# Packed attention and two MoE layers on one core: each engine's order of steps read from a table, the first batch's second-attention result split from SBUF, the coefficients loaded later

## The chip, the cores and the metric

One core of a Trainium2 chip runs the kernel. The metric is device time in microseconds (us), the median of three runs. The core has five engines that run their own instruction streams: PE (matmul, with weight loads listed as PEld), ACT, DVE, POOL and SP. In this kernel SP computes nothing: it issues the DMAs, one after the other, and a DMA whose data isn't there yet holds up all that stand behind it.

## The reference, cut to what matters

```python
batch, n_heads, seq, head_dim, n_pack = 8, 8, 576, 64, 32
n_tokens, d_model, d_ff = 4608, 512, 2048

def sm_attn(qq, kk, vv):
    s = scale * qq @ kk.T
    a = exp(s - max(s));  a = a / (sum(a) + 1e-09)
    return a @ vv

p_packed = sm_attn(p, k, v)                 # 32 rows a head
out = sm_attn(q, p_packed, p_packed)        # 576 rows a head
x = out.transpose(0, 2, 1, 3).reshape(4608, 512)

h = x @ w_in1                               # layer 1, w float64
P = a[0] + a[1]*h + a[2]*h**2 + a[3]*h**3
Q = 1 + |b[0]|*|h| + |b[1]|*h**2
x = (P / (Q + 1e-06)) @ w_out1

h = x @ w_in2                               # layer 2
out = (h * cos(h)) @ w_out2
```

## The kernel before

The attention is cut into 16 units (8 batches, two groups of four heads). A unit u transposes k, q and p on PE, makes the first softmax and from it the packed values, then the second softmax, whose weights, turned, stand in SBUF as `a2T` and are written to DRAM (`keep_attn`). The second product of the attention isn't made: `m_prod` multiplies the packed values into layer 1's `w_in` and gives a matrix M for a batch, so layer 1 starts from the softmax weights themselves.

Layer 1 runs over items j = 0 to 127: 16 half-batches c of 288 rows, eight items each. A product in float32 is made of three matmuls with operands split in a high and a low part (`..._hi` on ACT, `..._lo` on POOL or DVE). For each half-batch `a2_load` (L742) brings the softmax weights back from DRAM by two DMAs, one for each head group, `a2_hi` (L749, ACT) and `a2_lo` (L753, POOL) split them. Then for each item: `front` (L815, PE, 12 matmuls into one of two PSUM buffers `b`), `lin`, `absolute`, `slope` (ACT, L930, L944, L947), `cubic` (DVE, L939, L941), `denom` (POOL, L953), `log` and `inverse` (ACT, L956 and the next), `over` and `ratio` (DVE, L964, L968), `upper` (ACT, L996: the high part gh), `lower` (DVE, L999: the low part gl), and `back` (L852, PE, `acc<-gh,wo` and `acc<-gl,wo`). `front(j)` must wait until `cubic(j-2)` has read the PSUM buffer.

Layer 2 runs over items j = 128 to 271: nine chunks of 512 rows, 16 items each: `front` (L831), `lin` (L932), `rounded`, `reduced`, `clipped` (DVE, L972, L977, L979, L983), `cosine` (ACT), `times` (DVE, L990, the last reader of the PSUM buffer), `upper`, `lower`, and `back` (L852) in four steps m = 0 to 3. Its operand x comes from layer 1's output through DRAM: `x_load` (L895) and `x_rest` (L904) load the two sums of it, `x_sum` (POOL, L911) adds them, `x_hi` (L914, ACT) and `x_lo` (L918, DVE) split. Finished rows go by `done2` and `store` (L883).

The weights are float64 and come in as words: `w_load` (SP, L420, L425, L430), `w_exp` (L438) and `w_low` (L441, ACT), `w_abs` (L447) and `w_join` (L457, DVE), `w_hi` (L464, ACT), `w_lo` (L469, POOL). Layer 2's split `w_in` is written to DRAM (`keep_out`, L473) and loaded again (`w_back`, L476) while layer 1 ends, so weights of layer 2 are made beside the last items of layer 1.

What sets the order: every step is given to `plan.add` with its engine, its estimated length and what it reads and writes. `Plan.order` (L165 on) is a list scheduler: at each turn it takes, on the engine that can start first, that ready step with the least key among those that can start within 60 ns; a key is a sum of numbers found by tuning (`FIRST`, `EACH`, `WANTED`, `SHIFT`, by kind of step and place). Some steps also have to start behind others for the order alone (`after=`). The engines then get their instructions in this order, and semaphores keep the data right whatever the order is. The coefficients `par` (a[0..3], b[0..1]) are loaded by two DMAs ahead of everything (L1191, L1192).

Of the kernel before, what the change touches and what calls it, by code (L numbers as in the profile page):

```python
# [29 lines left out]
class Plan:  # L30
# [14 lines left out]
    WANTED = {  # L45
        "a2_hi": 1434, "a2_lo": 1536, "a2_load": -474, "absolute": -10, "absolute E": 828,
        "back 0": 407, "back 0 E": 574, "back 0 late E": 528, "back 1": 689, "clipped": 16,
        "copied k": 171, "copied k late": -117, "copied q": 61, "copied q late": 11, "cosine": -71,
# [3 lines left out]
        "exp_copied": -162, "exp_copied late": 137, "front 0": -336, "front 0 E": -21,  # L52
        "front 1": -170, "inverse": -79, "inverse E": 445, "keep_attn": -41, "keep_attn late": 15,
        "keep_out": 8, "keep_pack": -20, "keep_pack late": 229, "less_max2": -238,
        "less_max2 late": 87, "lin 0": 478, "lin 0 E": -611, "lin 1": -42, "load k": -478,
        "load k late": 78, "load p": -265, "load p late": -150, "load q": 49, "load q late": -161,
        "load v": -40, "load v late": -161, "log": 130, "log E": 244, "lower 0": -197,
        "lower 0 E": -245, "lower 1": 42, "m_hi": 793, "m_lo": -878, "m_load": 210, "m_prod": -188,
        "max1": -207, "max1 late": -84, "max2": -89, "max2 late": -237, "open_both": -151,
        "open_left": 19, "open_right": 88, "over 0": 25, "over 0 E": -124, "over 1": 23,  # L60
        "over 1 E": 120, "pack": 484, "pack late": 835, "packed": -18, "packed late": 191,
        "ratio": -8, "ratio E": -597, "recip1": 67, "recip1 late": 532, "recip2": 20,
        "recip2 late": 135, "reduced 0": -127, "reduced 1": -19, "rounded": 168, "scaled2": 114,
        "scaled2 late": 586, "scores 0": -176, "scores 0 late": -509, "scores 1": -379,
        "scores 1 late": -439, "slope": -18, "slope E": 518, "store": 300, "sum2": 80,
        "sum2 late": 1506, "taken p": -187, "taken p late": -160, "taken pp": 86,
        "taken pp late": -281, "times": -192, "trans k": -2, "trans k late": -333, "trans q": 692,
        "trans q late": -11, "turn2": -113, "turn2 late": -446, "turn_back": -189,
        "turn_back late": 1932, "turn_exp": 172, "turn_exp late": 219, "turned p": 73,
        "turned p late": 358, "turned pp": 24, "turned pp late": 59, "upper 0": 104,  # L70
# [13 lines left out]
    FIRST = {
        "i": 220.69, "j": 453.76, "k": 1649.06, "u": -144.84, "v": 113.95, "wi": -3610.16,
        "wi late": -1623.51, "wo": 597.92, "wo late": -1411.71,
    }
    EACH = {
        "i": 5.11, "j": 0.57, "k": 0.82, "u": -0.29, "v": 13.86, "wi": 0.11, "wi late": -1.42,
        "wo": -0.76, "wo late": -0.9,  # L90
    }
    SHIFT = {
# [63 lines left out]
    @staticmethod  # L156
    def kind(name, args):
        if name[:2] == "w_" and len(args) == 3:
            return f"{name} {args[0]} {args[2]}"
        if name in ("cubic", "over", "reduced", "trans", "copied", "turned", "taken", "load", "scores"):  # L160
            return f"{name} {args[1]}"
        if name in ("front", "back", "lin", "upper", "lower"):
            return f"{name} {int(args[0] >= 128)}"
        return name
# [1074 lines left out]
```

## Time and profile before

| | us |
|---|---|
| median of 3 runs (range) | 1619.49 (1619.04 to 1621.25) |
| the profiled execution | 1621.15 |
| its span, first to last instruction | 1619.4 |
| PE busy | 1553.7 (96%) |
| DVE busy | 1293.7 (80%) |
| ACT busy | 1032.1 (64%) |
| POOL busy | 344.0 (21%) |

The profiled execution lasts 1.75 us longer than its span and 1.66 us longer than the median. All rows below come from it. Lines L... are lines of the kernel before. In a timeline row the first number is the start (us from the span's start), the second the length of the group of instructions, then engine, line, operation, the tiles written and read, the shape and the number of instructions; the brackets give the idle time just before on that engine and what ended it. The program's parts follow in time: attention alone to some 65 us, attention and layer 1 to 150 us, layer 1 to about 800 us with layer 2's weights beside its last fifth, layer 2 from about 815 us.

### The profile page before, as it was taken

Reading aid. Unit: us, or ns where it says so; the run is one execution under the profiler, and the core shown is the slowest. Engines: PE = TensorE matmul, PEld = TensorE weight load, DVE = VectorE, ACT = ScalarE, POOL = GpSimd, SP = SyncE. Lnnn points to the kernel's source line nnn. Section 1 sums busy time; section 2 is a strip of 40 time slices with the busy share of each in tenths; the row PEclk is TensorE's granted clock in tenths of the full one; section 3 lists DMA queues with packets and bytes.
Section 4 is the critical chain, followed back from the end, with each engine's and each line's share of the span. In section 5 each row is a group of like instructions: output and inputs, shape, how many; then the busy total and the mean of one; then the engine's idle time right before and its main releaser. Section 6 shows DMA issues by size and latency. Waiting matters only on the chain.

```text
span 1619.4 us, 26741 instructions
## 1 busy us (share of the span) xinstructions
PE 1553.7 (96%) x10128; PEld 1335.3 (82%) x10128; DVE 1293.7 (80%) x2025; ACT 1032.1 (64%) x1745; POOL 344.0 (21%) x274
## 2 busy tenths in 40 slices
PE   5888998999999999999989999999999999999998
PEld 4566898789999999999878888888888788888887
DVE  4799999999999999998889876676676667666664
ACT  6898999989998888998767433333333333333332
POOL 1454442433343333333323100000000000000000
PEclk9999999999999999999999999999999999999999
DMA  9994115321221211134653310201010101010010
GB/s 307 334 318 152 63 48 168 102 75 50 74 80 52 67 64 62 43 104 139 200 161 119 82 35 13 53 20 46 14 39 14 39 1 43 10 31 22 1 27 27
DMA packets 98881, 133.61 MB, mean 83 GB/s; under 512 B 20928, under 2 KB 75712, under 8 KB 98752
## 3 DMA queue, kind: packets, MB, share of 16 engines
q1 hardware_dynamic: 98368, 131.38, 26.1%
q8 instruction: 80, 1.31, 0.3%
q10 hardware_dynamic: 384, 0.52, 0.1%
q14 instruction: 49, 0.40, 0.1%
HBM read 94.11 MB, written 37.75 MB: 81 GB/s over the span
## 4 chain that ended last, share of the span: by engine, by line
PE 76%; DVE 9%; ACT 8%; DMA 3%; issue 2%; POOL 2%; SPq 0%; DVEq 0%; POOLq 0%; ACTq 0%
PE acc L852 39%; PE b L831 24%; PE b L815 9%; PE b L765 2%; PE b L539 1%; DVE gl L999 1%; DVE T L964 1%; DMA raw<-in_moe_w_in_dram 1%; DMA k_in<-in_k_dram 1%; ACT T L930 1%; POOL U L953 1%; DVE T L941 1%; DVE T L939 1%; DVE T L968 1%; DVE U L964 1%
## 5 line engine op out<-in xcount | busy, mean ns | idle before, releaser
L852 PE MATMUL acc<-gh,wo 128*128 128x288 f32 x2048 | 420.1, 299 | 6.6 <-ACT ob L865 3.7
L852 PE MATMUL acc<-wo,gh 128*128 128x512 f32 x1152 | 354.9, 389 | 0.2
L852 PEld LDWEIGHTS acc<-gh,wo 128*128 128x128 f32 x2048 | 329.6, 189 | 29.6 <-issue 13.5
L852 PE MATMUL acc<-gl,wo 128*128 128x288 f32 x1024 | 302.6, 296 | 2.5 <-DVE gl L999 2.5
L953 POOL TENSOR_TENSOR U<-U,V 128x576 f32<-128x576 f32 x128 | 184.0, 1446 | 337.1 <-DVE T L964 90.6
L852 PEld LDWEIGHTS acc<-wo,gh 128*128 128x128 f32 x1152 | 216.0, 188 | 45.7 <-DVE xr L873 0.8
L932 ACT ACTIVATE T<-b 128x512 f32<-128x512 f32 x144 | 86.1, 598 | 219.2 <-PE b L831 218.4
L852 PE MATMUL acc<-wo,gl 128*128 128x512 f32 x576 | 224.4, 390 | 0.8 <-DVE gl L999 0.8
L999 DVE TENSOR_TENSOR gl<-V,gh 128x512 fp32r<-128x512 f32 x144 | 99.4, 690 | 122.5 <-PE acc L852 118.3
L852 PEld LDWEIGHTS acc<-gl,wo 128*128 128x128 f32 x1024 | 194.0, 189 | 3.5 <-DVE gl L999 3.5
L987 ACT ACTIVATE U<-U 128x512 f32<-128x512 f32 x144 | 90.8, 630 | 156.9 <-DVE U L983 156.8
L996 ACT CAST gh<-V 128x512 fp32r<-128x512 f32 x144 | 89.5, 621 | 76.3 <-PE acc L852 70.9
L972 DVE TENSOR_SCALAR T<-T 128x512 f32<-128x512 f32 x144 | 62.8, 436 | 91.2 <-ACT T L932 91.0
L852 PEld LDWEIGHTS acc<-wo,gl 128*128 128x128 f32 x576 | 108.1, 188 | 24.1 <-DVE gl L999 1.7
L947 ACT ACTIVATE U<-V,par 128x576 f32<-128x576 f32 x128 | 111.4, 870 | 1.3 <-DVE T L968 1.0
L990 DVE TENSOR_TENSOR V<-U,b 128x512 f32<-128x512 f32 x144 | 98.4, 684 | 17.2 <-ACT U L987 13.4
L999 DVE TENSOR_TENSOR gl<-T,gh 128x576 fp32r<-128x576 f32 x128 | 108.1, 846 | 4.5 <-PE acc L852 2.4
L930 ACT ACTIVATE T<-b,par 128x576 f32<-128x576 f32 x128 | 105.7, 831 | 4.8 <-PE b L815 4.0
L979 DVE SCALAR_TENSOR_TENSOR U<-T,U 128x512 f32<-128x512 f32 x144 | 105.2, 730 | 3.4
L964 DVE SCALAR_TENSOR_TENSOR U<-U,V 128x576 f32<-128x576 f32 x128 | 100.1, 786 | 8.0 <-POOL xr L911 4.3
L941 DVE SCALAR_TENSOR_TENSOR T<-T,par,b 128x576 f32<-128x576 f32 x128 | 102.0, 810 | 4.3 <-ACT V L944 1.7
L964 DVE SCALAR_TENSOR_TENSOR T<-T,par,V 128x576 f32<-128x576 f32 x128 | 105.1, 823 | 0.1
(182 smaller groups left out, 3077.3 us busy)
## 6 DMA issues: line engine op xcount, KB each, us to landing
raw<-in_moe_w_out_dram SPq DMA_DIRECT2D x32, 512.0 KB, 3.6
raw<-in_moe_w_in_dram SPq DMA_DIRECT2D x30, 512.0 KB, 4.6
x<-ob SPq DMA_DIRECT2D x24, 576.0 KB, 3.5
k_in<-in_k_dram SPq DMA_DIRECT2D x16, 576.0 KB, 7.4
q_in<-in_q_dram SPq DMA_DIRECT2D x16, 576.0 KB, 6.6
v_in<-in_v_dram SPq DMA_DIRECT2D x16, 512.0 KB, 7.2
w<-sc SPq DMA_DIRECT2D x32, 256.0 KB, 2.9
xr<-a SPq DMA_DIRECT2D x48, 144.0 KB, 3.4
```

Of the source, the lines that this page charges most:

```text
L815: nc.tensor.matmul(TILE["h", j][:, e, 0:HS], lhsT=w[:, o : o + P], rhs=x[:, g, :], start=n == 0, stop=n == 3 * NG - 1,)
L831: nc.tensor.matmul(h, lhsT=w[:, ks], rhs=x, start=n == 0, stop=n == 3 * KC - 1)
L852: nc.tensor.matmul(o, lhsT=w, rhs=x, start=i == first and n == 0, stop=i == last and n == len(todo) - 1,)
L930: nc.scalar.activation(T, hidden(j), AF.Identity, scale=par[:, 3:4], bias=par[:, 2:3])
L941: nc.vector.scalar_tensor_tensor(T, T, par[:, 1:2], h, op0=ALU.add, op1=ALU.mult)
L947: nc.scalar.activation(shaped(j, "U"), shaped(j, "V"), AF.Identity, scale=par[:, 5:6], bias=par[:, 4:5])
L953: return nc.gpsimd.tensor_tensor(Q, Q, V, op=ALU.mult)
L964: return nc.vector.scalar_tensor_tensor(t, t, add_, shaped(j, "V"), op0=ALU.add, op1=ALU.mult)
L979: return nc.vector.scalar_tensor_tensor(Y, T, -C2, Y, op0=ALU.mult, op1=ALU.add)
L987: nc.scalar.activation(Y, Y, AF.Sin, bias=PI/2)
L990: nc.vector.tensor_tensor(shaped(j, "V"), shaped(j, "U"), hidden(j), op=ALU.mult)
L999: return nc.vector.tensor_tensor(shaped(j, "gl"), result(j), shaped(j, "gh").bitcast(F32), op=ALU.subtract)
```

## The change

`Plan.order` no longer chooses: five lists of step numbers, `ORDER`, say for PE, ACT, DVE, POOL and SP which step comes next, and the loop only finds which slot each new tile gets. The keys and their numbers go, and so do those `after=` that were there for the order alone. The lists are near the old order, with steps moved singly. Three things change beside the order:

- `par_load` (two DMAs) and `par_abs` (ACT) become steps with a place in the lists. On SP they stand behind the first two weight loads, two p loads and two k loads.
- For the first batch (half-batches 0 and 1, first pass) `part_hi` and `part_lo` split the softmax weights from `a2T` in SBUF, 288 columns of one head group at a time. The four DMAs of `a2_load` for them, two `a2_hi` and two `a2_lo` of 576 columns go; four `part_hi` and four `part_lo` come. The store `keep_attn` remains.
- `logs[-1]` is now `inverse`, so that the cosine, which needs another function table on ACT, is put behind the last `inverse` and not the last `log`.

```diff
-    WANTED = {
-        "a2_hi": 1434, "a2_lo": 1536, "a2_load": -474, "absolute": -10, "absolute E": 828,
...
+    ORDER = {
+        "PE": """
+7 9 11 47 13 45 49 51 17 19 85 25 55 87 21 27 57 23 63 83 59 30 123 65 89 125 161 121 163 159
...
-        (group, i, off), s.kind = key, self.kind(fn.__name__, args) + late
-        s.base = (group, i, off)
-        key = self.FIRST[group] + self.EACH[group] * i + off + self.WANTED.get(s.kind, 0)
...
+        turn = {e: [self.steps[int(n)] for n in t.split()] for e, t in self.ORDER.items()}
+        turn["-"] = [s for s in self.steps if s.eng == "-"]
+        at = dict.fromkeys(turn, 0)
...
-                at = [(may(s), s) for s in ws]
-                first = min(a for a, _ in at)
-                if first == inf:
-                    continue
-                a, s = min(((a, s) for a, s in at if a <= first + self.WINDOW), key=lambda x: (x[1].key, x[1].n))
...
+                a = may(ss[at[e]])
+                if a < inf and (best is None or a < best[0]):
+                    best = (a, ss[at[e]])
...
+    def of_half(c, g):
+        return TILE["a2T", g][:, (c % 2) * HS : (c % 2 + 1) * HS]
+
+    def part_hi(c, g):
+        nc.scalar.copy(a2_parts(c, 0)[0][:, g, :], of_half(c, g))
+
+    def part_lo(c, g):
+        hi, lo = a2_parts(c, 0)
+        return nc.gpsimd.tensor_tensor(lo[:, g, :], of_half(c, g), hi[:, g, :].bitcast(F32), op=ALU.subtract)
...
+    def par_load():
+        nc.sync.dma_start(par[:, 0:4], rat_a.unsqueeze(0).to_broadcast([P, 4]))
+        nc.sync.dma_start(par[:, 4:6], rat_b.unsqueeze(0).to_broadcast([P, 2]))
...
-        if a == 0 or c < CE:
+        if b == 0 and a == 0:
+            for g in range(NG):
+                home = dict(w=[("a2", c, 0)]) if g else dict(new=[("a2", ("a2", c, 0), [P, 2, NG, HS], F32R)])
+                add("ACT", 290, at(j, -20), part_hi, c, g, tail=100, r=[("a2T", g)], **home)
+                add("POOL", 740, at(j, -20), part_lo, c, g, r=[("a2T", g)], w=[("a2", c, 0)])
+        elif a == 0 or c < CE:
...
-        add("ACT", 585, key, inverse, j, tail=100, w=[("V", j)])
+        logs[-1] = add("ACT", 585, key, inverse, j, tail=100, w=[("V", j)])
...
-    nc.sync.dma_start(par[:, 0:4], rat_a.unsqueeze(0).to_broadcast([P, 4]))
-    nc.sync.dma_start(par[:, 4:6], rat_b.unsqueeze(0).to_broadcast([P, 2]))
```

The order of the fronts on PE is as before; their places among the other PE steps shift by one to three steps on average. Three places are shown here. In the rows stand line, operation, tile written, tiles read and size; the numbers in the names tell one use of a buffer from another, and the lines of the changed code are other lines.

POOL near the end of layer 1 (some 790 to 805 us). L469, later L698, is `w_lo`; L953, later L1192, is `denom`; L911, later L1150, is `x_sum`. U1_10271 before and U1_10284 after belong to `denom(125)`. Before:

```order
L953 TENSOR_TENSOR U2_10163<-U2_10163,V2_10137 128x576
L469 TENSOR_TENSOR sc1_10378<-sc0_10256,sc2_10330 128x512
L911 TENSOR_TENSOR xr0_10053<-xr0_10053,xq_10259 128x512
L953 TENSOR_TENSOR U1_10271<-U1_10271,V1_10226 128x576
L953 TENSOR_TENSOR U0_10340<-U0_10340,V0_10313 128x576
L911 TENSOR_TENSOR xr1_10380<-xr1_10380,xq_10414 128x512
```

And now:

```order
L1192 TENSOR_TENSOR U0_10175<-U0_10175,V2_10167 128x576
L1192 TENSOR_TENSOR U1_10284<-U1_10284,V0_10262 128x576
L698 TENSOR_TENSOR sc0_10359<-sc1_10234,sc2_10356 128x512
L1150 TENSOR_TENSOR xr0_10294<-xr0_10294,xq_10229 128x512
L1192 TENSOR_TENSOR U2_10353<-U2_10353,V1_10297 128x576
L1150 TENSOR_TENSOR xr1_10051<-xr1_10051,xq_10399 128x512
```

`denom(125)` has moved ahead of one `w_lo` and one `x_sum`.

SP from about 813 us, where layer 2 begins. L473, later L702, is `keep_out`; L476, later L705, is `w_back`; L430, later L659, is `w_load` of layer 2's `w_out`; L895 and L904, later L1134 and L1143, are `x_load` and `x_rest`; L1107 is `x_out`. Before:

```order
L476 DMA m11h_10552<-w2_14_167 128x1024
L430 DMA raw1_10578<-in_moe2_w_out_dram 128x512
L473 DMA w2_15_168<-sc2_10576 128x512
L473 DMA w2_15_168<-sc1_10580 128x512
L476 DMA m11l_10635<-w2_15_168 128x1024
L895 DMA xr1_10662<-x20_1_130 128x64
L895 DMA xr1_10662<-x20_2_131 128x288
L895 DMA xr1_10662<-x20_3_132 128x160
L904 DMA xq_10674<-x21_1_146 128x64
L904 DMA xq_10674<-x21_2_147 128x288
L904 DMA xq_10674<-x21_3_148 128x160
L430 DMA raw0_10685<-in_moe2_w_out_dram 128x512
```

And now:

```order
L659 DMA raw1_10578<-in_moe2_w_out_dram 128x512
L1143 DMA xq_10595<-x21_1_146 128x64
L1143 DMA xq_10595<-x21_2_147 128x288
L1143 DMA xq_10595<-x21_3_148 128x160
L702 DMA w2_15_168<-sc2_10576 128x512
L702 DMA w2_15_168<-sc0_10601 128x512
L659 DMA raw0_10674<-in_moe2_w_out_dram 128x512
L659 DMA raw1_10698<-in_moe2_w_out_dram 128x512
L1107 DMA x20_15_144<-ob_10625 128x4x288
L705 DMA s6_10710<-w2_6_159 128x1024
```

Before, the load of `w2_15` (the row into m11l) stands straight behind the stores of it, and the next `w_out` load behind that and six x loads. Now the next two `w_out` loads follow the stores at once, and the load of `w2_15` stands twelve steps of the list later.

DVE at the same place. L447, later L676, is `w_abs`; L457, later L686, is `w_join`; L979, later L1218, and L983, later L1222, are `reduced` and `clipped` of item 129; L999 is `lower(128)`; L990, later L1229, is `times(129)`. Before:

```order
L979 SCALAR_TENSOR_TENSOR U0_10622<-T1_10611,U0_10622 128x512
L447 SCALAR_TENSOR_TENSOR sc1_10637<-sc0_10600,sc1_10637 128x512
L999 TENSOR_TENSOR gl0_10668<-V1_10632,gh0_10646 128x512
L457 SCALAR_TENSOR_TENSOR sc1_10637<-raw0_10491,sc1_10637 128x512
L983 TENSOR_SCALAR U0_10622<-U0_10622 128x512
L447 SCALAR_TENSOR_TENSOR sc0_10670<-sc2_10666,sc0_10670 128x512
L457 SCALAR_TENSOR_TENSOR sc0_10670<-raw1_10578,sc0_10670 128x512
L990 TENSOR_TENSOR V0_10690<-U0_10622,b2_1_10582 128x512
```

And now:

```order
L1218 SCALAR_TENSOR_TENSOR U2_10635<-T1_10616,U2_10635 128x512
L676 SCALAR_TENSOR_TENSOR sc0_10648<-sc1_10606,sc0_10648 128x512
L1222 TENSOR_SCALAR U2_10635<-U2_10635 128x512
L686 SCALAR_TENSOR_TENSOR sc0_10648<-raw0_10454,sc0_10648 128x512
L676 SCALAR_TENSOR_TENSOR sc1_10669<-sc2_10666,sc1_10669 128x512
L1229 TENSOR_TENSOR V1_10677<-U2_10635,b2_1_10582 128x512
```

`lower(128)` and one `w_join` have moved behind `times(129)`, and `clipped(129)` ahead of a `w_join`.

## Rows read from the trace of the kernel before

**Rows 1.** The page: busy time of each engine; the chain that ended last, by engine.

```profile
PE 1553.7 (96%) x10128; PEld 1335.3 (82%) x10128; DVE 1293.7 (80%) x2025; ACT 1032.1 (64%) x1745; POOL 344.0 (21%) x274
...
PE 76%; DVE 9%; ACT 8%; DMA 3%; issue 2%; POOL 2%; SPq 0%; DVEq 0%; POOLq 0%; ACTq 0%
```

**Rows 2.** Stretches: us, busy PE, PEld, DVE, ACT, POOL, PE clock, DMA share, GB/s.

```profile
10.40:50.00 39.60, 32.45 (x457) 21.73 (x465) 25.19 (x55) 29.69 (x61) 6.76 (x13) 0.96 1.05 339
50.00:100.00 50.00, 42.14 (x680) 29.04 (x664) 39.76 (x81) 44.49 (x89) 24.84 (x26) 1.00 1.02 344
100.00:150.00 50.00, 41.06 (x541) 32.05 (x541) 45.74 (x87) 44.75 (x86) 23.89 (x21) 0.97 0.69 234
150.00:350.00 200.00, 186.72 (x1473) 168.86 (x1473) 191.05 (x263) 181.33 (x298) 77.28 (x57) 0.98 0.27 85
350.00:750.00 400.00, 397.97 (x3105) 379.73 (x3104) 383.67 (x514) 364.74 (x590) 144.69 (x103) 1.00 0.23 75
750.00:850.00 100.00, 90.76 (x556) 83.17 (x555) 86.10 (x124) 73.44 (x123) 34.84 (x26) 0.97 0.51 164
850.00:1500.00 650.00, 648.45 (x2835) 527.85 (x2834) 450.31 (x780) 252.41 (x432) 30.98 (x26) 1.00 0.14 36
```

**Rows 3.** Stretches of 10 us in which the granted clock of PE is low.

```profile
280.00:290.00 10.00, 4.58 (x28) 3.13 (x28) 10.00 (x14) 8.21 (x13) 4.16 (x3) 0.71 0.38 127
...
800.00:810.00 10.00, 7.67 (x44) 7.44 (x45) 6.60 (x9) 3.52 (x6) 4.18 (x4) 0.83 0.46 151
```

**Rows 4.** Timeline, the start: coefficients, packs, first matmuls.

```profile
0.74 0.40 SPq L1191 DMA_DIRECT2D par<-in_moe_a_dram  x1
...
4.34 1.50 SPq L517 DMA_DIRECT2D p_in<-in_p_dram  x2
...
10.43 3.41 PE L539 MATMUL b<-ident,k_in 128*128 128x128 f32 x14 [10.43 <-DMA k_in<-in_k_dram]
```

**Rows 5.** DMA issues on the page: tiles, count, KB each, us to landing.

```profile
k_in<-in_k_dram SPq DMA_DIRECT2D x16, 576.0 KB, 7.4
...
xr<-a SPq DMA_DIRECT2D x48, 144.0 KB, 3.4
```

**Rows 6.** Timeline, 54 to 78 us: the first half-batch's split and first front.

```profile
66.47 1.40 POOL L753 TENSOR_TENSOR a<-xr,a 128x576 fp32r<-128x576 f32 x1 [4.00 <-ACT a L749]
...
69.32 0.53 PE L815 MATMUL b<-a,m00h 128*128 128x288 f32 x2
```

**Rows 7.** Groups by line and form: count, busy us, mean ns of one.

```profile
L749 ACT CAST a<-xr 128x576 fp32r<-128x576 f32 x24 | 16.2, 680 | 0.0
...
L865 ACT ACTIVATE ob<-acc 128x288 f32<-128x288 f32 x96 | 38.9, 409 | 3.7 <-PE acc L852 3.3
...
L753 POOL TENSOR_TENSOR a<-xr,a 128x576 fp32r<-128x576 f32 x24 | 34.4, 1433 | 23.8 <-PE acc L852 5.0 <-ACT a L749 4.0 <-DVE U L964 3.8
...
L469 POOL TENSOR_TENSOR wo<-sc,wo 128x512 fp32r<-128x512 f32 x32 | 41.1, 1289 | 83.3 <-DVE sc L457 17.5 <-ACT wo L464 11.9 <-DVE sc L447 10.2
```

**Rows 8.** Timeline, 275 to 290 us: the front of item 31.

```profile
285.42 0.82 PE L815 MATMUL b<-a,m00h 128*128 128x288 f32 x2 [5.50 <-DVE T L941]
```

**Rows 9.** Timeline, 790 to 836 us: from layer 1 to layer 2.

```profile
794.07 1.99 POOL L953 TENSOR_TENSOR U<-U,V 128x576 f32<-128x576 f32 x1
...
801.55 0.53 PE L852 MATMUL acc<-gh,wo 128*128 128x288 f32 x2 [2.77 <-ACT gh L996]
...
812.56 0.68 DVE L918 TENSOR_TENSOR a<-xr,a 128x512 fp32r<-128x512 f32 x1
...
825.97 0.98 PE L831 MATMUL b<-a,s 128*128 128x512 f32 x3 [1.66 <-DVE V L990]
...
830.00 0.66 ACT L438 ACTIVATE sc<-raw 128x512 f32<-128x512 f32 x1 [3.44 <-DMA raw<-in_moe_w_out_dram]
...
833.87 1.65 PE L831 MATMUL b<-a,s 128*128 128x512 f32 x3 [2.12 <-DVE V L990]
```

**Rows 10.** Timeline, the end: the last store.

```profile
1615.71 0.85 SPq L883 DMA_DIRECT2D out_dram<-xr  x2
```

More of the change, by code (lines that the diff above doesn't have):

```diff
@@ L43 @@
     RING, ISSUE = 8, 480
-    WANTED = {
-        "a2_hi": 1434, "a2_lo": 1536, "a2_load": -474, "absolute": -10, "absolute E": 828,
-        "back 0": 407, "back 0 E": 574, "back 0 late E": 528, "back 1": 689, "clipped": 16,
-        "copied k": 171, "copied k late": -117, "copied q": 61, "copied q late": 11, "cosine": -71,
[3 rows of a table removed]
[L52 to L70, printed above, removed]
[10 rows of a table removed]
-        "w_low 1 o": 16, "x_hi": 597, "x_lo": 263, "x_load": -65, "x_out": 179, "x_out E": 87,
-        "x_rest": 278, "x_sum": -47,
-    }
@@ L84 @@
[L84 to L92, printed above, removed]
[13 rows of a table removed]
-    }
-    PER = {"i": 4, "j": 8}
+    ORDER = {
+        "PE": """
[80 rows of a table added]
+""",
+        "ACT": """
[88 rows of a table added]
+""",
+        "DVE": """
[102 rows of a table added]
+""",
+        "POOL": """
[14 rows of a table added]
+""",
+        "SP": """
[18 rows of a table added]
@@ L154, in add @@
         return s
[L156 to L164, printed above, removed]
     def order(self):
         free = dict.fromkeys(("PE", "ACT", "DVE", "POOL", "SP", "-"), 0)
-        wait = {e: [] for e in free}
+        turn = {e: [self.steps[int(n)] for n in t.split()] for e, t in self.ORDER.items()}
+        turn["-"] = [s for s in self.steps if s.eng == "-"]
+        at = dict.fromkeys(turn, 0)
         free |= {"behind DVE": 0, "behind POOL": 0}
@@ L175, in order @@
         head = dict.fromkeys(self.slots_of, 0)
-        for s in self.steps:
-            if not s.left:
-                wait[s.eng].append(s)
         done = []
@@ L200, in order @@
             best = None
-            for e, ws in wait.items():
-                if not ws:
+            for e, ss in turn.items():
+                if at[e] == len(ss) or ss[at[e]].left:
                     continue
-                at = [(may(s), s) for s in ws]
-                first = min(a for a, _ in at)
-                if first == inf:
-                    continue
-                a, s = min(((a, s) for a, s in at if a <= first + self.WINDOW), key=lambda x: (x[1].key, x[1].n))
-                if best is None or a < best[0]:
-                    best = (a, s)
-            assert best, [(s.fn.__name__, s.args) for ws in wait.values() for s in ws][:40]
+                a = may(ss[at[e]])
+                if a < inf and (best is None or a < best[0]):
+                    best = (a, ss[at[e]])
+            assert best, [(s.fn.__name__, s.args) for e, ss in turn.items() for s in ss[at[e] : at[e] + 1]]
             a, s = best
-            wait[s.eng].remove(s)
+            at[s.eng] += 1
             s.start = a
             if s.eng == "SP":
-                n, at = s.busy // self.ISSUE, a
+                n, begin = s.busy // self.ISSUE, a
                 for _ in range(n):
-                    at = max(at, landed[-self.RING])
-                    bus = max(bus, at + 600) + s.bus / n
+                    begin = max(begin, landed[-self.RING])
+                    bus = max(bus, begin + 600) + s.bus / n
                     landed.append(bus + 1400)
-                    at += self.ISSUE
-                s.end, free["SP"] = bus + 1400, at
+                    begin += self.ISSUE
+                s.end, free["SP"] = bus + 1400, begin
             elif s.bus:
@@ L253, in order @@
                 t.left -= 1
-                if not t.left:
-                    wait[t.eng].append(t)
             done.append(s)
@@ L485, in convert @@
         bus = 1700 if x[::2] == (1, "i") else 1340
-        t = add("SP", 960 if (l, which) == (0, "i") and f % NPR == NPR - 1 else 480, (group, n, off - 4), w_load, *x, late=late, new=[("raw", ("raw", *x), [P, 2 * DM], U32)], bus=bus, after=[*after, *last_load[0]])
+        t = add("SP", 960 if (l, which) == (0, "i") and f % NPR == NPR - 1 else 480, (group, n, off - 4), w_load, *x, late=late, new=[("raw", ("raw", *x), [P, 2 * DM], U32)], bus=bus)
         last_load[0] = (t,)
@@ L1067, in operands1 @@
                     add("DVE", 1140, key, m_lo, b, n, g, tail=85, r=[("mps", b, n, g), ("M", b, n, g, "h")], w=[("M", b, n, g, "l")])
-        if a == 0 or c < CE:
+        if b == 0 and a == 0:
[4 more added lines that the diff above has]
+        elif a == 0 or c < CE:
             x = half(c, a * HALF)
-            add("SP", 960, at(j, -60), a2_load, c, x, r=[("a2 out", b * NG + g) for g in range(NG)], new=[("xr", ("a2r", c, x), [P, NG, HS], F32)], bus=880, after=[fronts[j - 7]] if j > 7 else ())
+            add("SP", 960, at(j, -60), a2_load, c, x, r=[("a2 out", b * NG + g) for g in range(NG)], new=[("xr", ("a2r", c, x), [P, NG, HS], F32)], bus=880)
             add("ACT", 570, at(j, -20), a2_hi, c, x, tail=100, r=[("a2r", c, x)], new=[("a2", ("a2", c, x), [P, 2, NG, HS], F32R)])
@@ L1085, in item1 @@
         add("ACT", 545, key, absolute, j, tail=95, r=[("h", j)], new=[("V", ("V", j), *W2P)])
-        add("ACT", 730, key, lin, j, tail=100, r=[("h", j)], new=[("T", ("T", j), *W2P)])
-        add("ACT", 760, key, slope, j, tail=105, r=[("V", j)], new=[("U", ("U", j), *W2P)])
+        add("ACT", 730, key, lin, j, tail=100, r=[("h", j), ("par",)], new=[("T", ("T", j), *W2P)])
+        add("ACT", 760, key, slope, j, tail=105, r=[("V", j), ("par",)], new=[("U", ("U", j), *W2P)])
         add("DVE", 665, key, cubic, j, 0, tail=85, r=[("h", j)], w=[("T", j)])
```

16 lines of the change are left out of this document (9 added, 7 removed), and 327 rows, old and new, of tables (ORDER, SHIFT, WANTED).

## The prediction

> **What bounds the kernel now.** I read the engines' shares first: PE is busy 1553.7 of 1619.4 us, so at most 65.7 us could be won by filling its gaps, and the chain that ended last runs through PE for 76% [rows 1]. Then the stretches, since such a share is a mean over parts with different limits [rows 2]. PE's idle time is each stretch less its busy time: 7.15, 7.86 and 8.94 us in the three stretches from 10.4 to 150 us (23.95 in all), 13.28 from 150 to 350, 2.03 from 350 to 750, 9.24 from 750 to 850, and 1.55 in the 650 us of layer 2. The start (10.4 us before PE's first matmul [rows 4]) and the tail hold the rest.
>
> Three different limits show. From 10 to 100 us the DMA engines are full (share 1.05 and 1.02, 339 and 344 GB/s). From 150 to 750 us DVE is nearly full too: 191.05 + 383.67 = 574.7 of 600 us, so it has 25.3 us to spare, 4%. Layer 2 is PE's alone. [...]
>
> **The change part by part.** The sum is made against the profiled execution, 1621.15 us; the median is 1.66 below it.
>
> *Start, 0 to 10.4 us.* The coefficients leave SP's front; two p loads take their place ahead of the k loads. PE's first matmul waits for k until 10.43. Two coefficient loads take some 0.8 us of SP (0.40 for the first), two p loads 1.50 [rows 4], so k is issued 0.7 us later, or its data come 0.7 to 1 us earlier if the order in which the bytes travel decides. The coefficients are needed by the first `lin`, past 69 us, so their delay is covered by 60 us. I take 0; bounds -1 to +0.9.
>
> *First batch's split.* Out go four DMAs of 144 KB, 0.58 MB: at 342 GB/s that is 1.7 us of a stream that is full. Each took 3.4 us to land [rows 5], a wait that the first split no longer has. In come instructions of half the width. ACT: one of 576 columns takes 680 ns, one of 288 (the nearest row is the eviction) 409; so 2 x 409 - 680 = 0.14 us more for each of two half-batches, 0.28 us. POOL: 1433 ns at 576 and 1289 at 512 columns give 2.25 ns a column, so 785 ns at 288, and 2 x 785 - 1433 = 0.14, 0.27 us for both [rows 7]. POOL is 50% busy there; ACT is 89% busy, so up to 0.28 us of it may show. The front that reads this split started at 69.32 with no wait noted, the split having ended at 67.87 [rows 6]: the shorter path alone wins nothing on PE, since the front keeps its place in PE's list. What is won is the DMA stream's 1.7 us, where loads of q, k and v end PE's waits.
>
> [...]
>
> *Order, 10 to 150 us.* All other steps shift singly by a few places. The 23.95 us are many waits of under 1.5 us: for q, k, v from DMA, for ACT's evictions. A list that fits can take a part, while the DMA stream sets a floor: it loses only 1.7 us of work. I take -3: 1.7 for the bytes, 1.3 from order; bounds 0 (the next load late instead) and -8 (a third).
>
> *Order, 150 to 350 us.* The one big stall is front(31): 5.50 us for `cubic(29)`'s second instruction [rows 8], and its slow clock: 10 us at 0.71 with 4.58 busy, so 4.58 x 0.29 = 1.3 us. In DVE's list one `w_join`, `cubic(30,0)` and `ratio(28)` have moved behind this `cubic` and one step ahead of it, about -1.3 us net. The other 7.8 us are small waits. I take -4 of 13.28; bounds 0 and -9.
>
> *350 to 750 us:* 2.03 us are left; -0.5.
>
> *750 to 850 us.* Three places. (a) `denom(125)` on POOL is now ahead of a `w_lo` (1.31 us there, 1289 ns mean) and an `x_sum`, 2.6 us. It ended at 796.06, its chain by ACT and DVE ended in gh, and `back(125)` waited 2.77 us for that [rows 7, 9]. This wait goes: -2.7. The matmuls behind it ran at a mean 0.83: 10 x 0.17 = 1.7 us that come back with the gap. But the next operand is `x_lo(0,1)`, which ended at 813.24 and which `front(128)` read with nearly no slack [rows 9]; its chain lies behind POOL and moves up by some 3 us only. So (a) nets -3.0. (b) `front(131)` waited 1.66 us for `times(129)`; `lower(128)` and one `w_join` (about 0.7 us each) are now behind it: -1.3. (c) `front(132)` waited 2.12 us for `times(130)`. On the way is ACT's wait of 3.44 us for `w_out` words [rows 9], whose load stood on SP behind the load of `w2_15`, and that behind its own stores' landing. Now the load follows the stores at once: up to -2.0; what frees DVE there also makes the next thing late, so of (b) and (c), 3.3 us, I take 2.0. Sum -5.0; bounds -1 (the x operands late as before) and -9.
>
> *Layer 2 to 1500 us:* 1.55 us idle in 650, PE paced by its own matmuls; shuffled steps m change nothing: 0. The cosine's new wait, for the last `inverse` rather than the last `log`, has ACT order behind it anyway: 0, as the first cosine comes behind both.
>
> *Tail.* The last items' `back` steps alternate, so stores drain evenly; the last store was issued at 1615.71, 0.85 us for two [rows 10]; with one fewer behind it, -0.7 (bounds 0 to -1.5).
>
> Sum: 0 - 3 - 4 - 0.5 - 5 + 0 - 0.7 = -13.2, so 1607.95 for a profiled execution, and 1606.3 by the median; I say 1606.5.
>
> **The rivals.**
>
> *DVE sets the pace, the waits only move.* DVE has 25.3 us to spare in 600 us, and no instruction leaves it. PE's wait for `cubic` is then DVE's queue seen from PE, and a step pulled ahead delays another by as much. What is left is half of the 750 to 850 part (DVE is 86% busy there) and nothing in the first 750 us: -2 to -2.5, 1617.5. For it: DVE's share; against it: PE still idles 13 us beside a DVE that itself idles 9 (200 - 191.05), so each waits for the other at times, which an order can mend.
>
> [...]
>
> *Larger gain.* The list also clears most small waits: 10 of the 23.95, 8 of 13.28, 1 of 2.03, 7 of 9.24 and 0.7: -26.7, some 1593 to 1597. Against it: the DMA floor in the first 100 us.
>
> *Slower: SP in a fixed order while DMA is full.* SP waits in order. Before, loads of things just stored stood well behind their stores: in the first 110 us the first `m_load` eight and `a2_load(2,0)` seven SP steps. Now they stand four and three behind, and the `w_load` of (0,3) of `w_out` stands five places earlier, ahead of the attention store `keep_attn(1)`, though it needs a buffer that a DVE step must free. With the stream full, a load takes 7.4 us to land (k) [rows 5]. If a store takes about as long, SP is held at each such place, and the next q, k and v loads are late by what exceeds the slack. It decides once SP is held longer than these 7.4 us, as loads in flight run out. Two such holds, each a stall like front(31)'s (5.5 us plus 1.3 us of clock), and none of the first 350 us' gain, leave 13.6 - 0.5 - 5 - 0.7 = +7.4; one, +0.6; I put the case at +4.5 on the median, 1624.
>
> **How the numbers follow.** Forecast (1600 to 1613) 0.56; larger gain 0.12; waits only move (1616.3 to 1622.7) 0.18; slower 0.14. That the change does nothing at all is inside the third. This measurement can tell about 0.2%, 3.2 us, from no change. So faster 0.68, same 0.18, slower 0.14. The range leaves out the tails of the larger gain and of the slower case: 1592 to 1622.
>
> **What would show it.** In the changed kernel's trace: no load into `xr` for the first two half-batches, and four ACT copies of about 410 and four POOL steps of about 785 ns; PE idle near 21 us from 10 to 150 us, near 9 from 150 to 350; no wait over 1 us for `denom(125)`'s chain, and a granted clock near 1.0 about 800 us; front(131) and front(132) with waits under 1 us; layer 2 as long as before. Wrong would be: SP's queue waiting several us for a DMA to land between 50 and 110 us, with PE behind it (the slower case); or DVE's busy share past 97% from 150 to 750 us with PE's idle time as before (the waits moved); or PE idle halved in the first 350 us (the larger gain).

## The result and the profile after

The changed kernel takes 1604.03 us in the median of 4 runs (1603.64 to 1605.03), against 1619.26 us for the kernel before, run four times beside it; the ratio is 0.9907, with a 95% interval from 0.9890 to 0.9924. The profiled execution lasts 1605.03 us, its span is 1603.2 us, so 16.2 us of span are gone. Forecast were 1606.5 us, in a range from 1592 to 1622.

The page of the kernel after (busy time by engine; the chain that ended last, by engine) answers [rows 1]:

```profile
PE 1546.9 (96%) x10128; PEld 1338.8 (84%) x10128; DVE 1276.8 (80%) x2025; ACT 1025.6 (64%) x1747; POOL 344.8 (22%) x276
...
PE 78%; DVE 8%; ACT 7%; DMA 4%; issue 2%; POOL 1%; SPq 0%; DVEq 0%; POOLq 0%; ACTq 0%
```

The stretches of the kernel after, in the columns of [rows 2]:

```profile
10.40:50.00 39.60, 31.52 (x452) 20.21 (x458) 24.05 (x51) 29.89 (x65) 7.38 (x9) 0.96 0.95 320
50.00:100.00 50.00, 41.45 (x629) 29.88 (x614) 37.22 (x78) 41.15 (x82) 22.18 (x27) 0.93 0.95 305
100.00:150.00 50.00, 43.46 (x600) 32.54 (x599) 45.98 (x89) 46.99 (x91) 25.89 (x23) 1.00 0.78 258
150.00:350.00 200.00, 185.86 (x1471) 168.83 (x1470) 186.88 (x264) 181.42 (x300) 78.84 (x59) 0.99 0.29 89
350.00:750.00 400.00, 399.44 (x3121) 381.41 (x3120) 382.92 (x520) 370.30 (x595) 144.43 (x103) 1.00 0.22 70
750.00:850.00 100.00, 94.08 (x573) 85.97 (x572) 87.53 (x132) 75.65 (x128) 35.27 (x27) 0.98 0.56 181
850.00:1500.00 650.00, 650.00 (x2867) 536.66 (x2866) 446.82 (x779) 243.31 (x428) 29.45 (x24) 1.00 0.13 35
```

Two things are to be seen. PE's busy time has *fallen* by 6.8 us with the same 10128 matmuls recorded, so a part of the old busy time was waiting, or matmuls at a slower clock. And from 850 to 1500 us PE ends 2867 matmuls where it ended 2835 before [rows 2]: 32 more in the same 650 us, although the idle time there went down by 1.55 us only.

Where the time went, by the start of the same step in both traces (us from the span's start). Between the marks PE's other steps have changed places, so the same mark doesn't always stand at the same work. Counted in the traces, from front(24) to front(118) PE has six matmuls of 288 columns more than before, from front(118) to front(140) six of 288 columns fewer and nine of 512 more, and from front(140) on nine of 512 fewer (3195 against 3204): nine matmuls of `back` now stand ahead of front(140). The column "at equal work" takes this out, with 0.133 us from one matmul of 288 columns to the next and 0.2267 us for 512.

| mark | before | after | gain so far | in this part | at equal work | forecast |
|---|---|---|---|---|---|---|
| first matmul on k | 10.43 | 8.82 | 1.6 | -1.6 | -1.6 | 0 |
| front(24) | 242.4 | 241.7 | 0.7 | +0.9 | +0.9 | -3, and part of -4 |
| front(118) | 744.2 | 742.9 | 1.2 | -0.5 | -1.3 | rest of -4, -0.5 |
| front(140) | 879.1 | 873.9 | 5.2 | -4.0 | -5.2 | -5 |
| end of the last matmul | 1614.3 | 1599.0 | 15.2 | -10.0 | -8.0 | 0 |
| end | 1619.4 | 1603.2 | 16.2 | -0.9 | -0.9 | -0.7 |

The sum came out near, 16.2 us against 13.2 forecast. Of its large terms only that of 750 to 850 us did: the first 350 us gave nothing where 7 us were forecast, and layer 2 gave eight where nothing was.

### The profile page after: what moved, and what is told of

Read it like the earlier page. It is cut to its first block, busy times and chain, and to the rows that moved or that the text cites. A ratio compares the mean times of both kernels' runs of the same rounds, so it can differ in the third digit from the quotient of the medians.

```text
span 1603.2 us, 26567 instructions
## 1 busy us (share of the span) xinstructions
PE 1546.9 (96%) x10128; PEld 1338.8 (84%) x10128; DVE 1276.8 (80%) x2025; ACT 1025.6 (64%) x1747; POOL 344.8 (22%) x276
## 4 chain that ended last, share of the span: by engine, by line
PE 78%; DVE 8%; ACT 7%; DMA 4%; issue 2%; POOL 1%; SPq 0%; DVEq 0%; POOLq 0%; ACTq 0%
PE acc L1091 42%; PE b L1070 24%; PE b L1054 9%; DMA raw<-in_moe_w_in_dram 2%; PE b L1004 2%; DMA q_in<-in_q_dram 1%; DVE T L1203 1%; DVE U L1203 1%; DVE gl L1238 1%; DVE T L1207 1%; DVE T L1178 1%; PE b L768 1%; ACT T L1169 1%; ACT U L1186 1%; DVE T L1180 1%
## 5 line engine op out<-in xcount | busy, mean ns | idle before, releaser
L1192 POOL TENSOR_TENSOR U<-U,V 128x576 f32<-128x576 f32 x128 | 183.2, 1441 | 340.6 <-DVE T L1207 115.7
L1229 DVE TENSOR_TENSOR V<-U,b 128x512 f32<-128x512 f32 x144 | 98.7, 685 | 62.6 <-ACT U L1226 61.3
L1238 DVE TENSOR_TENSOR gl<-T,gh 128x576 fp32r<-128x576 f32 x128 | 101.3, 793 | 7.8 <-PE acc L1091 5.8
L1178 DVE TENSOR_TENSOR T<-T,b 128x576 f32<-128x576 f32 x128 | 94.0, 747 | 13.1 <-ACT T L1169 9.5
L1218 DVE SCALAR_TENSOR_TENSOR U<-T,U 128x512 f32<-128x512 f32 x144 | 101.3, 704 | 2.8
```

The lines of the kernel that those rows point to most:

```text
L1178: nc.vector.tensor_tensor(T, T, h, op=ALU.mult)
L1192: return nc.gpsimd.tensor_tensor(Q, Q, V, op=ALU.mult)
L1218: return nc.vector.scalar_tensor_tensor(Y, T, -C2, Y, op0=ALU.mult, op1=ALU.add)
L1229: nc.vector.tensor_tensor(shaped(j, "V"), shaped(j, "U"), hidden(j), op=ALU.mult)
L1238: return nc.vector.tensor_tensor(shaped(j, "gl"), result(j), shaped(j, "gh").bitcast(F32), op=ALU.subtract)
```

## The experiments

All have the changed kernel's code; what changes is the table, or a line named. "The old order" is the order of the kernel before written out as a table. The ratios are to the kernel before, with their intervals; four kernels each ran on one chip together. Since the first 240 us scatter by some 4 us from one execution to the next (below), a part is also read by itself, in the one kept trace of each kernel, from the start of front(118) to that of front(140), and from there to the end of the last matmul. In the last column the old order of layer 2 (`before`, e1, e2, n1) has the nine matmuls more, 2.0 us, which are to be taken off before it is compared with the new; the new order has them in the column ahead of it.

| kernel | ratio (95%) | 118 to 140 | 140 to end |
|---|---|---|---|
| before | 1 | 134.95 | 735.2 |
| after, and the same as `a0_after` | 0.9908 (0.9893 to 0.9924) | 130.95, 130.87 | 725.2, 725.6 |
| `e1_old_order` | 1.0010 (0.9997 to 1.0024) | 134.53 | 736.8 |
| `e2_new_then_old` | 0.9960 (0.9946 to 0.9974) | 128.07 | 736.8 |
| `e3_old_then_new` | 0.9957 (0.9942 to 0.9972) | 134.46 | 725.6 |
| `e7_old_mid` | 0.9936 (0.9919 to 0.9953) | 136.85 | 725.2 |
| `n1_short_clip_old` | 1.0001 (0.9989 to 1.0014) | 133.29 | 732.8 |
| `n2_short_clip_new` | 0.9891 (0.9872 to 0.9910) | 130.92 | 724.7 |
| `n3_old_to24` | 0.9921 (0.9904 to 0.9938) | 129.40 | 725.3 |
| `a1_denom_late` | 0.9914 (0.9896 to 0.9933) | 132.69 | 725.6 |
| `b1_times129_late` | 0.9917 (0.9899 to 0.9935) | 135.97 | 725.2 |
| `c1_wback_behind_keep` | 0.9884 (0.9863 to 0.9904) | 130.70 | 725.8 |
| `f1_gl_early` | 0.9884 (0.9869 to 0.9900) | 130.24 | 725.7 |

### Order or code: e1

```diff
     ORDER = {
         "PE": """
-7 9 11 47 13 45 49 51 17 19 85 25 55 87 21 27 57 23 63 83 59 30 123 65 89 125 161 121 163 159 93
...
+9 11 47 7 49 45 13 51 17 19 55 57 25 85 27 87 63 21 65 23 59 30 83 123 121 89 125 127 161 93 95
...
```

> The changed code (split from SBUF, coefficients later, the cosine behind the last inverse) with the order of the kernel before written out as the table; the split's own steps stand where they are first ready. Theory 'the order carries the gain': near the kernel before, 1617 to 1619.5, since the 1.6 us won at the start and the 1.7 us of DMA bytes are given back in the first 150 us. Rival 'the code edits carry much of it', by the freed DMA stream: 1614 or less.

Measured: 1.0010, no gain. The split from SBUF and the later coefficients win nothing with the old order; what is won comes with the order.

### Which part of the order: e2, e3, e7, n3

In each the lists change over at a front, on all engines at once. e3 and n3 begin as e1 does; the first lines of PE that differ in e2, and then in e7, are

```diff
-3762 3774 3773 3776 3805 3788 3789 3819 3790 3803 3787 3802 3801 3833 3816 3804 3815 3847 3817
...
+3762 3774 3773 3776 3805 3788 3789 3819 3787 3790 3801 3802 3833 3803 3804 3847 3815 3829 3816
...
-3257 3258 3283 3281 3357 3284 3282 3383 3302 3299 3320 3301 3300 3319 3409 3318 3317 3427 3337
...
+3257 3258 3283 3281 3357 3284 3282 3383 3302 3299 3320 3301 3300 3319 3317 3318 3409 3427 3335
...
```

> The new order up to front(136), some 850 us, and the old order behind it. Theory 'layer 2's own order gives half the gain': between front(136) and the end the old order loses the 8 us that the two traces show there, so 1612 (1610.5 to 1613.5). Rival 'layer 2 is paced by PE's matmuls and its order is worth nothing', which was my term for it: 1604 to 1605.

> The old order up to front(136) and the new behind it. Theory 'layer 2's own order gives half the gain': 1619.3 - 8 = 1611 (1609.5 to 1612.5). Rival 'its order is worth nothing': 1618 to 1619.5.

> The new order but for the stretch from front(120) to front(136), some 752 to 850 us, which has the old one. Theory 'this stretch's order gives the 4.5 us that the traces show between 775 and 840 us, and layer 2 keeps them': 1608.5 (1607 to 1610). Rival 'the waits come back elsewhere, the stretch is worth little': 1604 to 1605.5.

> The old order up to front(24), some 240 us, and the new behind it. Theory from the two traces 'the first 240 us are worth nothing, waits have only changed place': within 1.5 us of the changed kernel. Rival, my sum, which gave 3 us to the first 150 us and a part of 4 us to the next 200: 3 to 5 us slower than the changed kernel.

> The changed kernel itself, the lists only broken into lines elsewhere, so that the others of this call stand beside it on the same chip: ratio 0.991 to the kernel before.

Measured against a0: e2 is 0.52% slower (8.4 us), and e3 0.53% faster than e1 (8.6 us): layer 2's order is worth 8 to 9 us, whatever stands ahead of it. Its time from front(140) on is 736.8 us with the old lists in both, so 734.8 at equal work, and 725.2 to 725.8 with the new in nine kernels. My rival, which was also my term, falls. e7 is 0.28% slower than a0 (4.5 us), as expected. The two intervals overlap, but the traces say the same: from front(118) to front(140), with the same matmuls, e7 takes 136.85 us, where the changed kernel takes 130.87 to 130.95 in its two traces and in n2's. So the stretch about 800 us is worth some 4.5 to 6 us, and layer 2 keeps it (725.2).

n3 is 0.13% slower, 2.1 us, with overlapping intervals; that decides nothing. Its trace and others tell a little more: front(24) starts at 240.1 to 244.0 us (mean 241.7) in the nine kernels with the new early order, at 242.8 to 248.1 (mean 245.9) in the four with the old early order and the new code, and at 242.4 in the one trace of the kernel before. By these the early part as a whole gains under 1 us; that the new code costs some us with the old early order and the new order makes up for them would fit, but with one trace of the kernel before it is not shown, and stays open.

### What layer 2 lost: n1, n2

```diff
         Y = shaped(j, "U")
+        Y = Y[:, 0:32] if j >= 134 else Y
         return nc.vector.tensor_scalar(Y, Y, -1.5 * PI, 0.5 * PI, op0=ALU.max, op1=ALU.min)
```

> The changed code with the old order, and in layer 2 from item 134 on the DVE step clipped works on 32 of its 512 columns (the rest goes unclipped to the cosine): some 0.33 us less between front(j) and the times(j) that frees the PSUM buffer for front(j+2); nothing else moves. Theory 'layer 2 loses its 8 us in the old order by fronts whose weight load waits a few tenths of a us for times': most of these waits end, so 5 us (3 to 7) less than the old order, ratio 0.997 to the kernel before. Rival 'the loss comes from the order of PE's own steps or from the table's other steps': 0 to 1 us less, ratio 1.000 to 1.001.

> The same short clipped from item 134 on in the changed kernel. Theory: its layer 2 has hardly a wait left (0.8 us over 750 us), so 0 to 1 us less than the changed kernel. Rival 'DVE's work as such sets layer 2's pace': the same gain as in the old order, 3 us or more.

The waits from 850 to 1590 us of PE's weight loads (PEld; us in total, times, longest) for `times`, first in the kernel before:

```profile
PEld b L831 <- DVE V L990: 12.3, 51, 0.6
```

then after:

```profile
PEld b L1070 <- DVE V L1229: 1.8, 9, 0.4
```

in e1, the old order with the new code:

```profile
PEld b L1070 <- DVE V L1229: 14.1, 51, 1.0
```

in n1:

```profile
PEld b L1070 <- DVE V L1230: 8.9, 37, 0.8
```

and in n2:

```profile
PEld b L1070 <- DVE V L1230: 1.0, 6, 0.2
```

A front's first weight load waits for the `times` that frees its PSUM buffer, 51 times by a quarter of a us, 12.3 us in all, and the page counts PE as busy over most of it: PE's own waits for `times` come to 0.4 us in the same stretch. With a `clipped` that is shorter by 0.24 us on average (0.43 to 0.19) the waits of the old order fall from 14.1 to 8.9 us, and front(140) to the end from 736.8 to 732.8: 4.0 us, inside the 3 to 7 expected. In the new order, with 1.8 us to win, the same cut gives 0.5 to 0.9. So it isn't DVE's work as such. Over e1, n1, after and n2 time goes with these waits: at equal work 734.8, 730.8, 725.2 and 724.7 us beside 14.1, 8.9, 1.8 and 1.0. n1's total doesn't show it: 1.0001 where 0.997 was expected, against e1's 1.0010, some 1.4 us with an uncertainty of 3. The early scatter can hide it, so this step rests on one trace of each kernel.

Why `times` was late before can be read in part from DVE's own waits from 850 to 1500 us; no run tests it. Before:

```profile
DVE gl L999 <- PE acc L852: 89.4, 53, 3.9
DVE T L972 <- ACT T L932: 82.9, 69, 3.8
DVE V L990 <- ACT U L987: 11.3, 15, 1.1
```

and after:

```profile
DVE T L1211 <- ACT T L1171: 108.4, 75, 3.7
DVE V L1229 <- ACT U L1226: 52.9, 70, 2.5
DVE gl L1238 <- PE acc L1091: 24.9, 16, 4.4
```

Before, DVE stood 53 times at a `lower` (L999) that waited for a buffer gl which a `back` on PE had to release, 89.4 us in all, and the next `times` was queued behind it: `times` started 2.1 us after the end of its cosine on average (over items 140 to 267). That is a part of the cause only. Of the 51 waits of the weight loads, 31 (6.6 of the 12.3 us) are for a `times` behind such a `lower`; 11 (3.4 us) are for a `times` that itself waited for the cosine, and the others for one behind other work of DVE. n1 took away the waits of these other kinds and left the 31, so it shows what a late `times` costs, and not what made it late.

After, 16 such waits of `lower` are left, `times` mostly waits for its cosine itself (70 times), and starts 0.54 us behind it. DVE's list hasn't moved `times` ahead of `lower` to get this: before, `times(k)` stands behind `lower(k-3)` in 116 of these 128 items, after in 57, and in 63 behind the still later `lower(k-2)`. What stands earlier is `back` on PE, which releases gl: when a front starts, PE is 5.25 items behind with `back` before and 4.0 after (median over items 141 to 270), and a front follows directly on another one 13 times, where it was 32. Which of these moves does how much wasn't tried. A front's start lies 0.26 us (median) behind the end of the `times` it needs in the kernel before, 0.84 us after.

### The stretch about 800 us: a1, b1, c1, f1

Each undoes one move of the changed kernel, or moves two steps more:

```diff
# a1, POOL: denom(125) behind w_lo and x_sum
-3577 3486 3504 3143 3582 3522 3587 3265 3540 3592 3381 3941 3601 3608 3615 3622 3629 3946 3636
+3577 3486 3143 3582 3504 3522 3587 3265 3540 3592 3381 3941 3601 3608 3615 3622 3629 3946 3636
# b1, DVE: lower(128) and w_join ahead of times(129)
-3724 3714 3725 3598 3726 3599 3605 3728 3606 3737 3716 3738 3739 3730 3740 3612 3751 3742 3752
+3724 3714 3725 3598 3726 3599 3605 3716 3606 3728 3737 3738 3739 3730 3740 3612 3751 3742 3752
# c1, SP: the loads of w2_14 and w2_15 (3573, 3574) behind their stores (3266, 3382)
-3405 3580 3259 3564 3144 3571 3569 3570 3586 3568 3590 3595 3591 3266 3567 3939 3572 3944 3602
-3940 3382 3609 3616 3557 3565 3623 3630 3945 3637 3644 3651 3658 3574 3949 3950 3665 3573 3672
+3405 3580 3259 3564 3144 3571 3569 3570 3586 3568 3590 3595 3591 3266 3573 3567 3939 3572 3944
+3602 3940 3382 3574 3609 3616 3557 3565 3623 3630 3945 3637 3644 3651 3658 3949 3950 3665 3672
# f1, DVE: lower(124) (3494) and lower(125) (3512) earlier
-3458 3140 3579 3474 3490 3491 3141 3492 3476 3521 3523 3539 3541 3508 3509 3494 3510 3262 3584
-3526 3527 3263 3528 3512 3530 3589 3545 3594 3544 3378 3546 3379 3548 3709 3710 3711 3723 3712
+3458 3140 3579 3474 3490 3491 3141 3492 3476 3521 3523 3539 3494 3541 3508 3509 3510 3262 3584
+3512 3526 3527 3263 3528 3530 3589 3545 3594 3544 3378 3546 3379 3548 3709 3710 3711 3723 3712
```

> The changed kernel with denom(125) on POOL behind that w_lo and that x_sum again, as before. My term (a): the time from the start of front(118) to that of front(140) grows by 2.6 to 3 us. Rival 'other waits stand at this place in the new order, for the low parts of items 124 and 125, and hide a part of it': 0 to 1.5 us.

> The changed kernel with lower(128) and one w_join on DVE ahead of times(129) again, as before. My term (b): front(131) waits 1.3 us longer, and front(118) to front(140) takes 1.3 us more (with a slower clock behind it up to 2). Rival 'DVE's other steps make up for it': 0 to 0.5 us.

> The changed kernel with the loads of w2_14 and w2_15 on SP straight behind their stores again, ahead of the w_out loads. My term (c): the w_out words come some 3 us later, ACT and DVE wait for them, front(132) waits some 2 us longer, and front(118) to front(140) takes 2 us more. Rival 'the words have slack in the new order': 0 to 0.5 us.

> The changed kernel with lower(124) three and lower(125) four places earlier on DVE, since PE waits 2.48 and 1.75 us for them near 793 and 799 us. Theory 'these two waits are what ate my term (a)': front(118) to front(140) takes 2 to 3 us less, and the whole as much less, which would be the fastest kernel. Rival 'the next operand is late anyway' (the x parts that front(128) and front(130) read): 0 to 1 us less.

PE's rows with a wait in the kernel after, from 790 to 830 us, answer [rows 9]:

```profile
794.56 0.40 PE L1091 MATMUL acc<-gl,wo 128*128 128x288 f32 x1 [2.48 <-DVE gl L1238]
...
799.77 0.45 PE L1091 MATMUL acc<-gl,wo 128*128 128x288 f32 x1 [1.75 <-DVE gl L1238]
...
822.07 0.98 PE L1070 MATMUL b<-a,s 128*128 128x512 f32 x3 [0.33 <-DVE V L1229]
...
828.13 0.98 PE L1070 MATMUL b<-a,s 128*128 128x512 f32 x3 [0.22 <-DVE V L1229]
```

The wait of 2.77 us for gh is gone, and two for gl, 4.2 us in all, have come. In a1 they are one:

```profile
797.48 0.61 PE L1091 MATMUL acc<-gl,wo 128*128 128x288 f32 x1 [5.60 <-DVE gl L1238]
```

so the early `denom(125)` is worth 5.60 - 4.23 = 1.4 us of wait, 1.8 us from front(118) to front(140): between my 2.6 and the rival's 1.5. In f1, with both low parts earlier, PE waits there for the high parts of the same items instead:

```profile
795.28 0.53 PE L1091 MATMUL acc<-gh,wo 128*128 128x288 f32 x2 [2.00 <-ACT gh L1235]
...
802.61 0.53 PE L1091 MATMUL acc<-gh,wo 128*128 128x288 f32 x2 [1.74 <-ACT gh L1235]
```

The next operand was late anyway. f1's 130.24 against 130.95 is less than the chance of the clock below: in f1 the granted clock was 1.00 from 790 to 810 us, and c1, with 1.00 too, took 27.1 us from front(126) to front(128) where f1 took 27.7. Nor is f1 a faster kernel that could be told apart (its interval overlaps a0's).

b1 costs 5.0 us where I expected 1.3. PE's wait in b1, and the stretch about it, with columns as above (the wait of the kernel after is shown above, 0.33 us):

```profile
826.53 1.65 PE L1070 MATMUL b<-a,s 128*128 128x512 f32 x3 [3.12 <-DVE V L1229]
```

```profile
822.00:832.00 10.00, 6.88 (x20) 5.14 (x19) 7.59 (x11) 5.09 (x10) 2.56 (x2) 0.69 0.61 206
```

The wait grew by 2.8 us, not 1.3: `lower(128)` doesn't only take its 0.6 us on DVE, it also waits there 1.50 us for its high part, and `times(129)` is queued behind it, as in layer 2. DVE in b1:

```profile
824.59 0.69 DVE L1238 TENSOR_TENSOR gl<-V,gh 128x512 fp32r<-128x512 f32 x1 [1.50 <-ACT gh L1235]
...
825.80 0.68 DVE L1229 TENSOR_TENSOR V<-U,b 128x512 f32<-128x512 f32 x1
```

And three matmuls then take 1.65 us where they take 0.98 after: the granted clock is 0.69 in this stretch, where the kernel after has 1.00 from 820 to 830 us, which leaves 2.2 us for the slower matmuls.

c1 costs nothing by its sum, but two effects cancel. front(131) waits 1.69 us (0.33 after), which is the cost; front(132) waits 0.23 as after, so the w_out words aren't what it waited for; and front(128) started 27.1 us behind front(126) instead of 28.65, by the clock (below). Against n3, which has the same order here and the same 27.2 us, c1 takes 1.3 us more.

```profile
822.40 0.96 PE L1070 MATMUL b<-a,s 128*128 128x512 f32 x3 [1.69 <-DVE V L1229]
...
828.41 0.97 PE L1070 MATMUL b<-a,s 128*128 128x512 f32 x3 [0.23 <-DVE V L1229]
```

## Why the prediction came out, and where its steps failed

**Start: 0 forecast, 1.6 us gained.** The step "two p loads 1.50" failed: they took 0.42 and 0.43 us, so k was issued at the same moment. Its data then came 1.6 us sooner, beyond my bound. PE's first matmul on k starts at 10.06 to 10.43 us in the five kernels with the old early order and at 8.41 to 9.21 in the nine with the new. That it is the coefficients' DMAs, which no longer go ahead, would fit; they weren't moved alone. ACT began on the first weight words 2.4 us sooner too, but their load was also issued 0.9 us sooner (0.74 against 1.66 us). Before:

```profile
2.60 1.69 SPq L527 DMA_DIRECT2D k_in<-in_k_dram  x2
...
7.35 0.66 ACT L438 ACTIVATE sc<-raw 128x512 f32<-128x512 f32 x1 [1.94 <-DMA raw<-in_moe_w_in_dram]
```

and after:

```profile
2.61 0.91 SPq L756 DMA_DIRECT2D k_in<-in_k_dram  x2
...
4.94 0.66 ACT L667 ACTIVATE sc<-raw 128x512 f32<-128x512 f32 x1 [2.92 <-DMA raw<-in_moe_w_in_dram]
...
8.82 3.44 PE L768 MATMUL b<-ident,k_in 128*128 128x128 f32 x14 [2.90 <-DMA k_in<-in_k_dram]
```

**10 to 150 us: -3 forecast, about +1 (read to front(24), at 242 us).** The step that failed is "the DMA stream sets a floor: it loses only 1.7 us of work". The bytes went, but the stream is no longer full: share 0.95 and 0.95, 320 and 305 GB/s, where it was 1.05 and 1.02, 339 and 344 [rows 2]. That is the kind of loss that the slower rival had, without its size. But SP's queue waited 78.6 us in all from 5 to 150 us, 5.6 us at the longest, and 78.4 and 5.3 us before, so it isn't shown that loads held up on SP are the reason.

**150 to 350 us: -4 forecast, nothing came.** PE idles 14.1 us there, 13.3 before. The stall of front(31) fell from 5.50 to 1.17 us, and the 10 us from 280 are at full clock:

```profile
285.10 0.50 PE L1054 MATMUL b<-a,m00h 128*128 128x288 f32 x2 [1.17 <-DVE T L1180]
```

```profile
280.00:290.00 10.00, 7.63 (x54) 6.96 (x52) 9.13 (x14) 8.83 (x16) 3.33 (x3) 1.00 0.39 131
```

But the slow clock has only moved: from 270 to 280 us the granted clock is 0.83, where it was 1.00 before, behind a wait of 1.99 us for an eviction. I had also priced it too low. All of the old kernel's 4.58 us of busy time from 280 to 290 lay at half clock (0.50 from 285.4 to 291 us), so the slow clock cost it some 2.8 us by 291, not 1.3; after, by the 0.83, 1.7. And other waits took the stall's place. PE's waits from 150 to 360 us, before:

```profile
PE b L815 <- DVE T L941: 8.2, 6, 5.5
PE acc L852 <- ACT ob L865: 2.7, 4, 1.7
```

and after:

```profile
PE acc L1091 <- ACT ob L1104: 6.4, 6, 2.0
PE b L1054 <- DVE T L1180: 2.7, 3, 1.2
PE b L1004 <- issue: 2.3, 2, 1.2
```

5.5 us less for `cubic`, 3.7 us more for ACT's evictions of the accumulators, 2.3 us new ahead of `m_prod`. I had priced the stall that goes and not what is late next; the rival "the waits only move" had this stretch right.

**350 to 750 us: -0.5 forecast.** PE ended 16 matmuls more (3121 against 3105 [rows 2]), at 0.133 us each 2.1 us. Again more than the idle time showed.

**750 to 850 us: -5 forecast, about 5 measured** (5.2 by front(118) to front(140) at equal work, 4.5 to 6 by e7). The parts: (a) 1.8 us against 3.0, as waits for gl came in place of the one for gh, and the clock that was to come back didn't (0.83 in the 10 us from 800 before and after); (b) 5.0 against 1.3, from 2.8 us more of wait and the clock behind it; (c) 1.3 against 2.0 for what (b) and (c) share, at front(131) and not at front(132). They overlap, so they don't add up to the whole. (a) was too large, (b) too small; that the whole is right is luck.

**Layer 2: 0 forecast, 8 us gained** (8.0 at equal work, 8 to 9 by e2 and e3). This is the step that failed most: "1.55 us idle in 650, PE paced by its own matmuls; shuffled steps m change nothing". The first half was read from a busy time that covers short waits. Rows I had told otherwise; these two are from the kernel before, at the start of layer 2:

```profile
814.57 1.52 PE L831 MATMUL b<-x,s 128*128 128x512 f32 x6
815.93 0.39 PE L831 MATMUL b<-a,s 128*128 128x512 f32 x1
```

Six matmuls of 512 columns without a wait take 1.36 us from the first's start to the next one's, 0.2267 us each, and 2835 of them [rows 2] need 642.7 of the 650 us. 7.3 us were lost there, and the 32 matmuls more are these 7.3 us. So the busy time of matmuls was a poor measure here of how near PE was to its limit: with these 32 matmuls it rose by 1.55 us only, that of the weight loads by 8.8, from 527.85 to 536.66.

**Tail: -0.7 forecast, -0.9 measured,** from the end of the last matmul to the end: 5.1 us before, 4.2 after.

So the forecast of faster was right, but that the total came near is luck: two errors of 7 and 8 us cancel. The signs I had named say so too. The granted clock about 800 us wasn't near 1.0, PE idled 14.1 us from 150 to 350 us and not 9, and layer 2 wasn't as long as before; what came were the shorter waits of front(131) and front(132), and four POOL steps of 798 ns where I had 785. The larger-gain and the slower case weren't met as wholes; the third, waits that only move, was true of the first 350 us.

## What to carry to other kernels

Where a profile shows PE full, count its matmuls in the stretch and multiply by the time from one to the next: what is missing to the stretch's length is lost, even if the idle column is near zero (7.3 us of 650 in the kernel before, beside 1.55 idle), and the waits of the weight loads say to whom. Before two marks are compared, count the matmuls between them too: a step that has changed places looks like a gain. In a fixed order, an instruction that waits holds up those behind it, as `lower(128)` did in b1, which waited 1.50 us. At front(131) it was enough to put `times`, which frees the scarce PSUM buffer, ahead of a `lower` that waits (b1, with a `w_join`: 5.0 us); in layer 2 the waits of `lower` went with an earlier `back`, so look at what releases the wait as well as at what stands behind it. A big stall that goes is priced with the wait that is late next at the same place, and not by its own length.
